# A new hand-written program order for one-core block-sparse attention followed by a gated feed-forward layer

## The chip, the cores and the metric

The kernel runs on 1 core of one Trainium2 chip. The metric is device time in microseconds for one execution. The kernel before takes 278.68 us (median of 3 runs, 277.92 to 278.79).

## The reference

The input is q, k and v in float32, each (4 batches, 8 heads, 768 positions, 64 dimensions), a table of three sampled key blocks for each of 24 query blocks, and three weights. Attention is dense in its arithmetic and masked by blocks of 32; the feed-forward layer reads the attention output as 3072 tokens of 512 features.

```python
scores = (1/8) * q @ k.T
mask = |blk_i - blk_j| <= 1  or  first/last block row or column  or  sampled block
attn = softmax(where(mask, scores, -1e9)) @ v        # (4, 8, 768, 64)
x = attn.transpose(0, 2, 1, 3).reshape(3072, 512)
gate = sigmoid(x @ w_gate)                           # w_gate, w_val: 512 x 1536
out = (gate * (x @ w_val)) @ w_out                   # w_out: 1536 x 512
```

All of it is computed. The sigmoid is taken as a tanh of half the argument, and the factor 1/2 is applied when the output leaves PSUM. Masked scores are made zero after the exponential by a product with a 0/1 mask, except for the first unit, where a bias is added by matmuls before the exponential.

## The kernel before

**Tiling.** The work has 12 units: batch b (0 to 3) by a third u of the queries (256 queries). A unit has 4 pairs of heads. For each pair there are three steps of 256 keys each:

- `scores` on TensorE: 4 matmuls of 64x128 weights (kT) by 256 columns of qT, two in parallel on the two halves of the array's rows; in the first unit 8, with the bias.
- `exp` on ScalarE: 128x1024 elements out of PSUM, to a buffer P.
- `mul` on VectorE: P times the mask (not in the first unit).

Then `pv` (units 0 and 1, whole array, 24 matmuls) or `pv_parts` (later units, half the rows each, 48 matmuls) forms P times v with a column of ones for the sum; `fold` (VectorE) adds the two halves, `norm` (VectorE) divides. The result is transposed to xT, for units 0 and 1 by TensorE with a copy out of PSUM (`turn`, `evac`), later by a DMA transpose from SP's queue (`xbar`).

The feed-forward part has 8 groups of units. A task `f` makes 512 columns of gate and value: a first half and a second half of 16 or 8 matmuls each (the first group in one piece on the whole array), then `tanh` on ScalarE and `gate` on VectorE, which frees the PSUM unit. A task `y` makes 256 output tokens in six parts of 8 matmuls, two evacuations and two stores from SP's queue. The last unit's output (`y_last`) is split in three so that the last evacuation is small.

**Preparation.** Batch 0's k and q come in as two heads at a time, are transposed by TensorE and copied out of PSUM by VectorE or ScalarE (`prep.turn`, `prep.evac`); the block mask is expanded by small matmuls (`mask_tiles`) and copied to SBUF. Later batches are loaded on POOL's queue, paired on VectorE (`pair_up`) and transposed by DMA on SP's queue; v is copied to a padded buffer on VectorE (`vcopy`). The first loads stand in a fixed list, `FIRST`, and are not touched here.

**Order.** All engines' programs follow from one list, `ORDER`. Every piece of work is a task with a number; `Plan.run` goes through the tokens and issues each task's instructions on its engine. A token is a task number, an optional engine letter (P, A, D, G, S) that replaces the task's first choice, `:n`, which of the four PSUM units it takes, and `@m`, a gate: this load waits until task m has run. `jN` is a filler of two matmuls on zeros into unit N (`jNs` a short one). Each engine runs its own instructions strictly in this order; semaphores come from data and buffers. There are four PSUM units of two banks, and a task that takes a unit waits until the evacuation of its last owner is done. So a token's place decides three things: what is behind it on its engine, when a unit comes free, and when a load starts.

The task numbers that the prediction speaks of are: 126, 127, 132, 133, 147, 171, 176, 190 (f of the first group); 204 to 206 (first y); 34, 32, 44, 40, 36, 30, 64, 56, 60, 46, 50, 54 (scores of the first unit); 38, 48, 58, 93 (their pv); 14, 19, 24, 29 (their v copies); 15/16, 17/18, 20/21, 22/23, 25/26, 27/28 (transposes of batch 0 and their copies); 74 to 85, 97/98, 106/107, 117/118 (mask matmul and its copy); 138/139 and 152/153 (pair copy and DMA transpose of k and q of batch 1, pair 0), 229/230 (k of pair 2); 268 and 318 (scores of batch 1, pairs 0 and 2); 1148 to 1157 (y of unit 10), 1158 to 1172 (y_last); 1097 and 1099 (the stores of unit 9's output).

Of the kernel before, what the change touches and what calls it, by code (L numbers as in the profile page):

```python
# [24 lines left out]
DM = H * D  # L25
# [20 lines left out]
122:3 85A 113 140:0 127 123 91 130:1 128 132:3 141 129 131 72:2 119:0 99:1 73D 133 120 147:2 134  # L46
100 135 142 157:0 148 154:3 171:1 124 155 149 158 88 164:3 143:2 156 176:0 92@164 144 121 146@111
101 172 170@44 165 173 161:2 217@54 145 190:1 177 189@46 162 125@40 178 237@54 159 186:3 191 150:2
115:0 151D 192 174:2 187 116 204:1 175 188 231:0 179:3 183:2 232 205 180D 244:3 184 233 206 166
245 82:0 200:2 218 83D 201 246 234:3 193:0 219 194A 152 235 185 153 211:2 136:0 220 137D 212 138  # L50
272:3 195 139 229 223A 202 167:0 255:2 168 236 273 213 221A 239 214:0 230 307:1 274 169 215 275
256 240 216 197:3 308 257 196 181 198 258 248:0 309 182 199 241:2 249 242 310 268:3 262 225:1 250
260 114@268 263 269 251 252:2 226 318:0 261 207:3 319 253 315:1 208 289:2 316 160@315 254 106:0
265:3 243 290 107A 247@265 266 270 276:1 209 291 300:0 293:3 277 301 278 282:1 294 292 283 297 163
303:0 335:2 295 302 222 304 279 227 285:1 336 296 286 238 359:0 305 337 360 210 284 331:3 228
362:1 348 332 361 264 349 363 333 328:0 287 350 329 267 322:3 351A 320 344:1 353A 311:0 323
203@344 345 341:2 387:3 321@359 312 342 317 271@282 426:1 373:0 313 411@300 427 330 397:2 374 398
343 388 346 375 259 408:1 376 389 355:2 400@268 409 390 347@30 419:0 356 334@89 380:3 405:1 428
370:2 381 306@111 364 420 288@44 406 371 386@214 366:3 421 410 365@265 454:2 422 433:1 455 432@380
# [3 lines left out]
442 474:1 484:0 463A 378 465A 339 467:2 452 340 475 524:3 480 485 525 514 354 515:1 327 468 486  # L63
# [4 lines left out]
538 583 438 550:1 567 571 542 439 586 551 638:0 563:2 572 425 539 564 552 595:1 573A 404 577:2 604  # L68
639 574 596 578 609:0 568 597 555 575A 627:2 598 616:3 610 628 617 543@616 635:1 565 712@200 630:2
611 569@300 636 612 592:3 446@563 688:0 631 593 658@60 689 654 706:1 556@231 588:3 707 579 641@550  # L70
640 642:0 632 676@471 619:1 633 589 587@282 620 594 691@214 623:2 690 613 590 670:1 591 643 671
637 605:3 624 644 621 606 645 659:1 618 625 709:0 681:3 710 626 660 607 655:2 682 692:0 656 453
663:3 711 726@99 661 657 608@234 673:2 693 662 674 622@652 664 672 694 548 699:1 695 665 723:2 666
# [3 lines left out]
762 669 782 730:3 745A 734:0 760 757:2 731 735 753 798:3 703 758 799 732 736 764:0 759 750 743A  # L77
600 765 797 826:3 823:1 767 763 824 650 816:0 766 651 827 809:1 756 768 810 719 800 787:3 817 769
733 788 806:1 801:0 807 770D 819:3 789 772A 811 737:1 790:2 839 738 614 802 580 615 791 803 601
# [5 lines left out]
904 856 925 936:0 978:1 913 937 911 857 919:3 979 908 875:0 920 914 876 929:1 921 917A 905 932  # L85
970:3 930 935 971 877 922 946:0 915A 1024:3 931 947 893 1025 928 1027:2 1012:0 939 938 916 1013
948 959:3 1028 966 1040:0 940 960 1041 1026 941 967:2 973:3 944A 942D 968 945 1029 952:0 1001:1
# [6 lines left out]
1078 1074 1094 1008 1082 1095 1083 1084 1100:1 1087A 1096A 1108:3 1088 1098A 1101 1085A 1099 1097  # L94
# [3 lines left out]
1163:2 1154D 1164 1159 1156D 1155 1157 1165 1160 1166 1167 1168:0 1161 1169 1170 1162 1171 1172  # L98
"""
GAP, PV_HALF, PV_PARTS, F_HALF, Y_ONE = 0.3, 0.36, 0.74, 0.875, 0.216  # L100
# [56 lines left out]
def kernel(  # L157
# [246 lines left out]
    t_mb = plan.add([(DVE, 0.7)], mask_blocks)  # L404

    def rows(c1, fn, engines):

        bank = Bank()

        def mm(eng):  # L410
            for i, c0 in enumerate(range(0, c1, 512)):
                c = slice(c0, min(c1, c0 + 512))
                nc.tensor.matmul(
                    both(bank)[:, i, 0 : c.stop - c0], mb16, e64[0:D, c], start=True, stop=True
                )

# [13 lines left out]
        [(DVE, 0.42)],  # L430
    )
    t_rows = [
        rows(S, lambda eng, spread: copy(eng, mb24, spread), [(DVE, 0.95), (ACT, 0.82)])
    ]

    def mask_tiles(c0, c1, j):
# [14 lines left out]
        def evac(eng):  # L451
# [3 lines left out]
        a = plan.add([(PE, n / 4800)], mm, t_rows, take=bank, ops=4)  # L455
        return plan.add(
            [(DVE, 0.12 + n / 860), (ACT, 0.16 + n / 1180)], evac, [a], free=bank
# [20 lines left out]
    def prep(nm, src, dst, b, p, t0, t1):  # L478
# [32 lines left out]
        if staged is None:  # L511
            c = plan.add([(PE, 0.04 * n)], turn, take=bank, ops=8 * n)
            copies.setdefault((nm, b, p), []).append(c)
        else:
            a = plan.add([(DVE, 0.1 + 0.14 * n), (ACT, 0.2 + 0.14 * n)], pair, before("pr", i))
# [7 lines left out]
    def pair_up(nm, src, dst, b, p, deps):  # L523
        def go(eng):
            nc.vector.tensor_copy(
                dst[:, p, :, :, :],
                src[:, 2 * p : 2 * p + 2, :, :].rearrange("a h t d -> a t h d"),
            )

        a = plan.add([(DVE, 0.36)], go, deps)  # L530
        copies.setdefault((nm, b, p), []).append(a)
        return a

# [624 lines left out]
```

## Time and profile before

| | |
|---|---|
| runs | 277.92, 278.68, 278.79 us |
| profiled execution, span from first to last instruction | 277.8 us (the page gives no other time of it) |
| mean granted clock of TensorE | 0.999 |
| TensorE busy | 270.0 us (97%) |
| VectorE busy | 207.1 us (75%) |
| ScalarE busy | 192.1 us (69%) |
| POOL busy (issuing loads) | 47.3 us (17%) |
| DMA | 28.93 MB, mean 104 GB/s |

In the profile PE is TensorE's matmul, PEld its weight load, DVE VectorE, ACT ScalarE. A row names the source line, the engine, the operation and its tiles. Matmuls overlap: a row's length is from issue to the modelled end, so two rows that start 0.11 us apart may each be 0.27 long, and TensorE's pace is read from starts. A table by windows has for each stretch its length, then the busy time of each engine, and at the end the granted clock, the mean share of DMA and GB/s. In a timeline the columns are start and length in us; square brackets hold the engine's idle time before the row and what ended it.

### The profile page before, as it was taken

To read this page: it belongs to the slowest core of one execution; us is meant where nothing else is said; L and a number is where in the kernel's file an instruction comes from. 1 tells how busy PE (TensorE), PEld (TensorE's weight loads), DVE (VectorE), ACT (ScalarE), POOL (GpSimd) and SP (SyncE) were. 2 spreads that over 40 slices of the span, in tenths; PEclk is the share of its full clock that TensorE was granted. 3 is DMA by queue.
4 is the path that set the end of the run, shared out by engine and by line. 5 is a ranking of instruction groups with operands and counts; after the bars stand their busy time and mean duration, and the time that the engine had idled before them with its cause. 6 is when DMAs were issued, how large, how long until landed. Compare 5 with 4: busy or idle time off the path is not lost.

```text
span 277.8 us, 11169 instructions
## 1 busy us (share of the span) xinstructions
PE 270.0 (97%) x5007; PEld 178.7 (64%) x5007; DVE 207.1 (75%) x421; ACT 192.1 (69%) x243; POOL 47.3 (17%) x69
## 2 busy tenths in 40 slices
PE   8879999999999999999999999999999999999995
PEld 3667785896897798655566655655655676555543
DVE  4667788899999989978988886887876899004422
ACT  3988868899989958968868965679688571035300
POOL 7776261030480000028300000000000000000000
PEclk9999999999999999999999999999999999999999
DMA  7999999994599693339986743014130002230004
GB/s 160 175 195 197 200 205 198 140 139 100 84 160 145 117 140 97 103 98 167 142 113 113 73 61 97 2 21 142 24 96 4 4 2 76 70 151 2 0 2 151
DMA packets 56684, 28.93 MB, mean 104 GB/s; under 512 B 33036, under 2 KB 53692, under 8 KB 56636
## 3 DMA queue, kind: packets, MB, share of 16 engines
q0 software_dynamic: 21520, 13.90, 35.7%
q1 hardware_dynamic: 34628, 14.02, 24.8%
q8 instruction: 39, 0.64, 1.0%
q10 hardware_dynamic: 488, 0.30, 0.3%
q14 instruction: 9, 0.07, 0.1%
HBM read 28.47 MB, written 6.29 MB: 125 GB/s over the span
## 4 chain that ended last, share of the span: by engine, by line
PE 87%; DMA 7%; POOL 2%; ACT 1%; DVE 1%; issue 1%; SPq 0%
PE m L352 86%; DMA q<-in_q_dram 3%; DMA v<-in_v_dram 2%; DMA kT<-kp 1%; ACT P L586 1%; POOL k L226 1%; POOL q L226 1%; POOL wg L236 0%; POOL wv L236 0%; DVE ysb L888 0%; DVE P L592 0%; ACT ysb L886 0%; PE m L472 0%; PE m L467 0%; ACT ysb L929 0%
## 5 line engine op out<-in xcount | busy, mean ns | idle before, releaser
L586 ACT ACTIVATE P<-m 128x1024 f16<-128x1024 f32 x144 | 143.1, 1025 | 27.8 <-PE m L352 24.6
L352 PE MATMUL m<-xT,wg 64*128 64x512 f16 (+2 forms) x720 | 136.7, 326 | 0.1
L352 PE MATMUL m<-xT,wv 64*128 64x512 f16 (+2 forms) x720 | 136.7, 326 | 0.0
L592 DVE TENSOR_TENSOR P<-P,mask 128x1024 f16<-128x1024 f16 x132 | 87.0, 684 | 2.7 <-ACT P L586 2.6
L352 PEld LDWEIGHTS <-wg 64*128 64x128 f16 (+1 forms) x720 | 66.6, 94 | 21.2 <-issue 0.8
L352 PEld LDWEIGHTS <-wv 64*128 64x128 f16 (+1 forms) x720 | 66.4, 94 | 18.2 <-issue 0.5
L804 DVE SCALAR_TENSOR_TENSOR ht<-th,m 128x512 f16<-128x512 f32 x72 | 49.0, 685 | 37.0 <-ACT th L801 36.1
L352 PE MATMUL m<-wo,ht 64*128 64x512 f16 (+2 forms) x564 | 70.4, 372 | 0.0
L801 ACT ACTIVATE th<-m 128x512 f32<-128x512 f32 x72 | 42.8, 598 | 29.6 <-PE m L352 26.1
L352 PE MATMUL m<-qT,kT 64*128 64x256 f16 x576 | 53.6, 269 | 0.9 <-DMA kT<-kp 0.5
L352 PEld LDWEIGHTS <-P 64*128 64x128 f16 (+1 forms) x2112 | 41.1, 94 | 5.2 <-issue 0.4
L352 PEld LDWEIGHTS <-ht 64*128 64x128 f16 (+1 forms) x564 | 29.4, 94 | 23.4 <-issue 1.3
L352 PE MATMUL m<-vex,P 64*128 64x65 f16 (+1 forms) x2112 | 42.5, 190 | 0.0
L352 PEld LDWEIGHTS <-kT 64*128 64x128 f16 x576 | 26.7, 94 | 17.8 <-issue 1.3
L646 DVE TENSOR_REDUCE acc<-m 128x260 f32<-128x520 f32 x40 | 27.8, 697 | 7.9 <-PE m L352 6.8
L226 POOL DMA_DIRECT2D k<-in_k_dram x15 | 11.1, 744 | 48.3 <-PE m L352 45.0
L886 ACT ACTIVATE ysb<-m 128x512 f32<-128x512 f32 x18 | 10.2, 601 | 11.8 <-PE m L352 11.8
L656 DVE TENSOR_TENSOR x<-acc,rz 128x256 f16<-128x256 f32 x40 | 17.0, 425 | 1.4
L226 POOL DMA_DIRECT2D v<-in_v_dram x16 | 11.6, 736 | 33.5 <-PE m L352 12.9
L226 POOL DMA_DIRECT2D q<-in_q_dram x19 | 13.9, 733 | 3.9 <-DMA wo<-in_moe_w_out_dram 1.8
L352 PE MATMUL m<-bias,e 64*128 64x256 f16 x48 | 5.9, 271 | 2.3 <-DVE mask L299 1.9
L929 ACT ACTIVATE ysb<-m 128x256 f32<-128x256 f32 x1 | 0.4, 383 | 10.1 <-PE m L352 10.1
(47 smaller groups left out, 84.1 us busy)
## 6 DMA issues: line engine op xcount, KB each, us to landing
out_dram<-ysb SPq DMA_DIRECT2D x23, 256.0 KB, 2.4
v<-in_v_dram POOLq DMA_DIRECT2D x16, 192.0 KB, 5.1
k<-in_k_dram POOLq DMA_DIRECT2D x15, 192.0 KB, 6.6
q<-in_q_dram POOLq DMA_DIRECT2D x12, 192.0 KB, 6.4
wg<-in_moe_w_gate_dram POOLq DMA_DIRECT2D x6, 256.0 KB, 8.4
wv<-in_moe_w_val_dram POOLq DMA_DIRECT2D x6, 256.0 KB, 9.0
wo<-in_moe_w_out_dram POOLq DMA_DIRECT2D x3, 512.0 KB, 12.8
xT<-x SPq DMA_TRANSPOSE x40, 2.4
```

The source lines that it names most:

```text
L226: return nc.gpsimd.dma_start(dst[:, h0:h1, t0:t1, :], src[b, h0:h1].rearrange("h (p t) d -> p h t d", t=NT)[:, :, t0:t1, :],)
L352: return nc.tensor.matmul(out, lhsT, rhs, start=start, stop=stop, skip_group_check=True).ins
L586: nc.scalar.activation(self.pt.rearrange("a h i n -> a (h i n)"), both(self.bank).rearrange("a h n -> a (h n)"), AF.Exp, bias=0.0, scale=SCALE
L592: nc.vector.tensor_tensor(self.pt, self.pt, m.unsqueeze(1).broadcast_to([128, 2, 2, UQ]), op=ALU.mult,)
L646: nc.vector.tensor_reduce(self.acc.rearrange("a h s d -> a (h s d)"), self.parts.rearrange("a r n -> a n r"), axis=mybir.AxisListType.X, o ...
L656: nc.vector.tensor_tensor(self.x16.rearrange("a s h d -> a h s d"), self.acc[:, :, :, 0:D], rz.broadcast_to([128, 2, 2, D]), op=ALU.mult,)
L801: nc.scalar.activation(th, both(bank)[:, 0, :], AF.Tanh, bias=0.0, scale=0.5)
L804: nc.vector.scalar_tensor_tensor(self.ht[:, tiles[0] : tiles[-1] + 1, :], in0=th.rearrange("a (f n) -> a f n", n=self.w), scalar=1.0, in1= ...
L886: nc.scalar.activation(ysb, both(bank)[:, s, :], AF.Copy, bias=0.0, scale=0.5)
L929: nc.scalar.activation(ysb, src, AF.Copy, bias=0.0, scale=0.5)
```

## The change

Only `ORDER` changes what runs: the order of all engines, the PSUM unit of each task, the engine of some copies and the gates of the loads are new. The tasks themselves, and so the matmuls, exponentials, products, copies, loads and stores, are the same. Beside it, the numbers for durations and the labels in the `plan.add` calls are replaced; they are notes for whoever writes the order, and `Plan.run` reads none of them but the engine letter of the first choice and the bank to take.

Counted in the two lists: filler pairs go from 19 to 13. Output evacuations go from 18 on ScalarE and 4 on VectorE to 14 and 8; mask copies from 3 and 6 to 2 and 7; transposed copies of xT in the first units from 1 and 7 to 3 and 5; copies of k and q in the first batch from 1 and 12 to 2 and 11, and the 768-column mask rows go from VectorE to ScalarE. All 36 later loads have a gate in both. The changes of the array's tile shape along TensorE's order are 43 in both.

```diff
 ORDER = """
-j3 j3 j3 j3 j3 j3 j3 j3 5A 8D j3 0 11A j3s 9:0 j3s j3s j3s 10D j3s j3s 12:1 1:2 j3s 13A 3:0 2 j3s 34:1 4D 35 15:2
-j3s 32:3 16D 6:0 33 17:1 7D 117:2 18D 97:0 118D 44:1 98A j3s 22:3 78:2 23D 45 36:0 79D 20:3 37 21D
-40:2 25:1 30:3 41 26D 76:0 77D 46:1 31 54:2 19 74:0 47 75D 27:3 24 55 50:0 28D 80:1 64:3 51 81D
-48:2 65 60:1 49 56:0 61 14 66:3 58:2 67D 105@30 57 29 89:3 59 38:1 90 52:0 86:2 53D 87 39 68:3
-93:0 69D 62:1 108:2 94 42:3 109 43D 102:0 63D 111:3 70:1 103 110 126:2 71D 112 104 95:0 84:1 96D
...
-1115 1126 1136:0 1127 1117 1121 1118 1132:1 1122 1137 1123 1119 1128:3 1138 1133 1139 1144:2 1134
-1140:0 1135 1129 1145 1130 1141 1131 1146 1148:1 1147 1142 1149 1143 1150 1158:3 1151 1152 1153
-1163:2 1154D 1164 1159 1156D 1155 1157 1165 1160 1166 1167 1168:0 1161 1169 1170 1162 1171 1172
+0 5A j3 j3 j3 j3 j3 j3 j3 j3 j3s 6:0 11 8A j3s j3s 9:1 10 12:2 1:3 2 13 7A 3:0 4A j1s j1s 15:3 16A
+34:2 84:0 85 92@34 32:1 17:3 18 97:0 35 98 33 44:3 45 22:2 23 78:0 40:1 41 25:2 79 36:0 37 27:3
+30:1 28 26 74:3 75 31 64:2 65 20:0 21 76:3 77 56:1 57 14 60:0 46:2 47 38:3 19 39 48:1 50:2 61 49
+51 42:3 29 54:0 55 43 66:1 67 93:3 24 86:1 80:2 87 105@86 99:0 100 94 81 58:3 167:1 168 217@167 59
+82:2 83 68:0 146@167 69 164:3 165 95:2 96 52:1 53 102:0 62:2 63 111:1 108:3 126:2 103 166 109 112
+70:0 71 127 89:3 128 129 90 140:0 141 132:1 113 119:3 120 72:2 104 133 134 122:0 73 237@122
...
+943 1096D 1082 1083 1084 1085 1087 1104:0 1116:1 1086 1105 1106 1107 1117 1118 1098D 1124:2 1128:0
+1140:3 1129 1141 1119 1130 1131 1142 1143 1100:1 1112:0 1101 1108:3 1113 1102 1103 1114 1132:1
+1088 1115 1109 1110 1111 1125 1120:0 1136:3 1121 1126 1127 1144:2 1133 1122 1123 1134 1135 1137
+1138 1139 1145 1146 1148:1 1149 1147 1150 1163:2 1151 1152 1153 1156 1157 1164 1158:3 1154 1097
+1159 1160 1165 1161 1099 1162 1155 1168:1 1169 1170 1171 1172 1166 1167
 """
```
```diff
-        a = plan.add([(PE, c1 / 2200)], mm, [t_mb], take=bank, ops=2 * (1 + (c1 > 512)))
+        a = plan.add([(PE, c1 / 2400 + 0.003)], mm, [t_mb], take=bank, mode="Q", needs=("c0", "e0"))
...
-        return plan.add([(SP, 1.25)], go, deps, dma=("T", 0))
+        return plan.add([(SP, 1.29)], go, deps, dma="T")
...
-                [(ACT, 0.98)], st.exp, [a] + before("P", 3 * pr.i + st.j), free=st.bank
+                [(ACT, 0.903)], st.exp, [a] + before("P", 3 * pr.i + st.j), free=st.bank
```

More of the change, by code (lines that the diff above doesn't have):

```diff
@@ L429 @@
         ),
-        [(DVE, 0.42)],
+        [(DVE, 0.335)],
     )
     t_rows = [
-        rows(S, lambda eng, spread: copy(eng, mb24, spread), [(DVE, 0.95), (ACT, 0.82)])
+        rows(S, lambda eng, spread: copy(eng, mb24, spread), [(DVE, 0.87), (ACT, 0.70)])
     ]
@@ L454, in mask_tiles @@
         n = 2 * (c1 - c0)
-        a = plan.add([(PE, n / 4800)], mm, t_rows, take=bank, ops=4)
+        a = plan.add([(PE, n / 4800 + 0.003)], mm, t_rows, take=bank, needs=("e0", "e1"))
         return plan.add(
-            [(DVE, 0.12 + n / 860), (ACT, 0.16 + n / 1180)], evac, [a], free=bank
+            [(DVE, 0.065 + n / 960), (ACT, 0.054 + n / 1200)], evac, [a], free=bank
         )
@@ L548, in go @@
             )
-        a = plan.add([(DVE, 0.4)], go, deps + read.get(("pv", b - 2, p), []))
+        a = plan.add([(DVE, 0.268)], go, deps + read.get(("pv", b - 2, p), []), needs=(f"v{p}",) if b == 0 else ())
         copies.setdefault(("v", b, p), []).append(a)
@@ L692, in value @@
                 a, free = plan.add(
-                    [(DVE, 0.66)], self.fold, [a] + folded[-3:-2], free=self.bank
+                    [(DVE, 0.609)], self.fold, [a] + folded[-3:-2], free=self.bank
                 ), None
             self.normed = plan.add(
-                [(DVE, 0.6 if free else 0.5)], self.norm, [a] + before("x16", self.i), free=free
+                [(DVE, 0.55)], self.norm, [a] + before("x16", self.i), free=free
             )
@@ L722, in xt @@
                 plan.add(
-                    [(DVE, 0.29), (ACT, 0.37)],
+                    [(DVE, 0.203), (ACT, 0.268)],
                     self.evac,
@@ L744, in scores @@
         a = plan.add(
-            [(PE, (0.44 if first else 0.22) * len(run))],
+            [(PE, (0.433 if first else 0.217) * len(run))],
             mm,
@@ L748, in scores @@
             take=run[0][1].bank,
-            ops=16 if first else 8,
+            score=True,
+            needs=("e0", "e1") if first else (),
         )
@@ L758, in scores @@
                 continue
-            pr.products.append(plan.add([(DVE, 0.66)], st.mul, [e] + masks[st.j, st.u]))
+            pr.products.append(plan.add([(DVE, 0.599)], st.mul, [e] + masks[st.j, st.u]))
         return a
@@ L844, in f @@
                     take=bank,
-                    lag=GAP,
-                    ops=16 * self.per,
+                    needs=wneeds,
                 )
                 a = plan.add(
-                    [(PE, F_HALF)], half(False), [a], ops=16 * self.per
+                    [(PE, 0.863 if self.w == 512 else 0.872)], half(False), [a], turn=True
                 )
             used["xT"][self.g].append(a)
-            c = plan.add([(ACT, 0.57)], tanh, [a] + before("th", i), free=bank, part=1)
-            g = plan.add([(DVE, 0.68)], gate, [c], free=bank, part=1)
+            c = plan.add([(ACT, 0.477)], tanh, [a] + before("th", i), free=bank)
+            g = plan.add([(DVE, 0.598)], gate, [c], free=bank)
             used["th"][i] = [g]
@@ L898, in part @@
                     take=bank if first and f0 == 0 else None,
-                    lag=0.0 if f0 < 8 else GAP if first else None,
-                    ops=16,
+                    turn=not first and f0 == 0,
+                    needs=(f"o{f0 // 4}",),
                 )
@@ L911, in y @@
                 e = plan.add(
-                    [(ACT, 0.6), (DVE, 0.69)],
+                    [(ACT, 0.477), (DVE, 0.605)],
                     lambda eng, s=s: evac(eng, s),
@@ L940, in store @@
                 [after],
[L941 removed]
+                dma="O",
             )
```

122 lines of the change are left out of this document (58 added, 64 removed), and 40 rows, old and new, of the table ORDER.

## The prediction

> **What bounds the kernel now.** I read, in this order, the page's shares and chain, the table by windows, the chain in order of time, and then the timelines of TensorE, ScalarE and VectorE for the first 25 us. The page first: TensorE's busy share and its share of the chain that ended last.
>
> ```profile
> PE 270.0 (97%) x5007; PEld 178.7 (64%) x5007; DVE 207.1 (75%) x421; ACT 192.1 (69%) x243; POOL 47.3 (17%) x69
> PE 87%; DMA 7%; POOL 2%; ACT 1%; DVE 1%; issue 1%; SPq 0%
> L586 ACT ACTIVATE P<-m 128x1024 f16<-128x1024 f32 x144 | 143.1, 1025 | 27.8 <-PE m L352 24.6
> ```
>
> TensorE is the bound, and the change leaves its work alone. So a new order can win only where TensorE waits. The windows (length in us, then busy time of each engine) show where that is.
>
> ```profile
> 4.60:16.00 11.40, 8.90 (x223) 6.59 (x221) 8.04 (x18) 8.88 (x11) 9.50 (x14) 1.00 1.31 178
> 16.00:24.00 8.00, 7.48 (x203) 5.83 (x201) 5.35 (x17) 7.22 (x8) 5.43 (x8) 1.00 1.45 197
> 42.00:110.00 68.00, 68.00 (x1628) 54.87 (x1624) 62.17 (x128) 59.54 (x74) 11.47 (x16) 1.00 0.88 132
> 110.00:125.00 15.00, 14.47 (x308) 8.95 (x302) 12.54 (x26) 12.17 (x16) 1.52 (x3) 1.00 0.38 100
> 125.00:200.00 75.00, 75.00 (x1404) 44.21 (x1402) 63.09 (x127) 56.80 (x71) 7.81 (x11) 1.00 0.54 87
> 200.00:210.00 10.00, 9.88 (x150) 5.72 (x146) 7.91 (x14) 8.67 (x11) 0.00 (x0) 1.00 0.24 74
> 265.00:277.80 12.80, 9.68 (x76) 5.01 (x70) 2.73 (x5) 0.38 (x1) 0.00 (x0) 0.98 0.22 83
> ```
>
> From 42 to 200 us TensorE rests only once, 0.53 us in all, and once more between 200 and 210. The rest of its idle time lies in the first 24 us (2.50 and 0.52) and in the tail (3.12, of which about 3.1 is the last evacuation and store). Busy hides something: a row's time includes the pipeline's drain, so starts must be read as well. The chain in order of time names the two waits in the middle and the end.
>
> ```profile
> 114.71 2.86 ACT P L586 x3
> 117.60 0.69 DVE P L592
> 118.29 0.28 DVE vex L545
> 118.66 4.07 DMA kT<-kp
> 204.92 0.60 ACT ysb L886
> 205.55 0.70 DVE ysb L888
> 274.71 0.38 ACT ysb L929
> ```
> ```profile
> 121.35 0.90 PE L352 MATMUL m<-vex,P 64*128 64x65 f16 x48
> 122.78 0.39 PE L352 MATMUL m<-qT,kT 64*128 64x256 f16 x3 [0.53 <-DMA kT<-kp]
> ...
> 205.80 0.38 PE L352 MATMUL m<-qT,kT 64*128 64x256 f16 x4
> 206.30 0.37 PE L352 MATMUL m<-xT,wg 64*128 64x512 f16 x1
> ```
>
> At 118 us a transpose of k for the next batch is issued late, behind VectorE's queue, and its landing at 122.7 holds the scores of task 616. At 205 us two evacuations of one output unit run one behind the other, and FFN half 1001, which takes that unit, waits for the second. The second fence gives TensorE's own starts there. The 48 value matmuls at 121.35 take 0.73 where the next task follows at once, so 1.43 - 0.73 = 0.70 is lost; the score at 205.80 takes 0.22 of its 0.50, so 0.28 is lost.
>
> **The start, step by step.** The timeline of ScalarE, then VectorE and TensorE, in the first 25 us (start, length, instruction, idle time before it):
>
> ```profile
> 6.73 1.94 ACT L586 ACTIVATE P<-m 128x1024 f16<-128x1024 f32 x2 [0.86 <-PE m L352]
> 8.56 0.59 ACT L297 CAST mask<-m 128x512 f16<-128x512 f32 x1
> 9.17 5.69 ACT L586 ACTIVATE P<-m 128x1024 f16<-128x1024 f32 x6
> 16.01 4.82 ACT L586 ACTIVATE P<-m 128x1024 f16<-128x1024 f32 x5 [1.15 <-PE m L352]
> 22.61 2.85 ACT L586 ACTIVATE P<-m 128x1024 f16<-128x1024 f32 x3 [0.55 <-PE m L467]
> ```
> ```profile
> 6.42 0.27 PE L352 MATMUL m<-qT,kT 64*128 64x256 f16 x2
> 6.62 0.38 PE L472 MATMUL m<-const,k 64*64 64x64 f16 x24
> 14.35 0.36 DVE L545 COPY vex<-v 128x768 f16<-128x768 f16 x1 [1.53 <-DMA v<-in_v_dram]
> 15.36 0.29 PE L352 MATMUL m<-bias,e 64*128 64x256 f16 x2 [1.91 <-DVE mask L299]
> 15.47 0.29 PE L352 MATMUL m<-qT,kT 64*128 64x256 f16 x2
> 16.47 0.79 PEld L352 LDWEIGHTS <-P 128*128 128x128 f16 x24 [0.21 <-issue]
> 23.94 0.28 PE L352 MATMUL m<-xT,wg 128*128 128x256 f16 x1
> 41.20 0.39 PE L352 MATMUL m<-wo,ht 64*128 64x512 f16 x2
> ```
>
> Six exponentials in 5.69 us, the last 1.025 long, are (5.69 - 1.03) / 5 = 0.93 us apart. A pair of 256-column matmuls starts 0.11 after the one before (15.36, 15.47), so a score costs 0.22 and a score of the first unit, with its bias, 0.44. A change of tile shape costs about 0.1 (weights at 16.47, 0.11 later than the pairs' pace); both orders have 43 of them, so they drop out. The before order puts the copy of v for pair 1 (19) on VectorE ahead of a mask copy (75). The v load was late, VectorE waited 1.53 us, the mask copy kept its PSUM unit, and TensorE waited 1.91 us at task 50. The first FFN task (126) begins at 23.94.
>
> The new order moves the v copies (14, 19, 29, 24) behind all mask copies that hold a unit, so this wait goes. What is late next is ScalarE. It gets two larger copies ahead of the first exponential (4A, the 768-column mask rows, and 16A, the transposed k of pair 1, whose transposes ran at 6.62 before), about 0.7 us each by the 0.59 that the 512-column copy takes. I walk it through: first exponential at 7.6 instead of 6.73; 16 exponentials at 0.93 are 14.9; and about 0.5 of idle time, because score 50 waits for the unit of exponential 47 behind two value products (38, 48). The sixteenth (165) then ends at 7.6 + 14.9 + 0.5 = 23.0. Task 108, which takes its unit, costs 0.2 and the hand-over and change of tile shape 0.1: task 126 starts at 23.3, 0.64 earlier. Ahead of it TensorE has also done more: scores 99, 167, 164, masks 82 and 84 and a transpose (0.93 us) come in, score 89, mask 117 and the transpose 70 (0.58) go out. So the lead is 0.64 + 0.35 = 1.0 us there. Up to the first output task (204) part of it is given back: scores 119 and 122 and FFN task 147 take units whose exponentials (90, 141, 120) end only as TensorE arrives. Counted in start-to-start lengths, 204 has 29.63 us of TensorE work ahead of it in the new order and 28.83 in the old; my walk puts it at 41.35 against 41.20: a lead of 0.80 - 0.15 = 0.65. I take **-0.65**; the ends are 0, if ScalarE idles 0.65 more, and -1.6, if its 0.5 of idle time and the hand-backs vanish. That the fillers fall from 19 to 13 pairs costs nothing: they run where TensorE waits anyway.
>
> **The middle.** The k and q transposes of later batches are reached with 10 to 50 us of TensorE work to spare (the tightest, 393, 10.7; before, 439 had 9.9 and was the one that stalled), and the unit after an output's evacuations (801, 387) is taken with 0.4 to 0.5 us to spare. Both waits, 0.70 and 0.28, go: **-0.98** (ends 0 and -1.04).
>
> Against that, the new order hands PSUM units over tighter. A score's matmul that starts at 6.42 has its partner at 6.53 and its exponential at 6.73: 0.20 of hand-over, then 1.025, so a unit can be retaken about 1.26 us of TensorE time after its score. In the new order eight takes lie at 1.29 (584 after 653, 524 after 496, and so on); before, none was under 1.5. Takes with less than 0.5 us to spare are 24 beyond the first 50 us, against 8. I walked 41 to 68 us with the rows' lengths and found the new order waiting 0.05 us in all; the slips must come from lengths that vary. I take **+0.3**; the ends are 0 and 24 x 0.1 = 2.4.
>
> Loads: all 36 keep a gate, at other places. POOL's queue gets batch 2's first load (271) behind score 186, about 44 us by my walk, where before it came behind the v load 203 and its gate 344, some 25 us of TensorE work later; VectorE's pair copies for it come earlier too. SP's queue then carries batch 1's transposes 139 and 153 at 44.4 and 45.8 us, while loads still run. The issue list gives their time to landing (median us at the end):
>
> ```profile
> xT<-x SPq DMA_TRANSPOSE x40, 2.4
> qT<-qp SPq DMA_TRANSPOSE x12, 4.2
> kT<-kp SPq DMA_TRANSPOSE x12, 3.3
> ```
>
> By 4.2 the second lands at 50.0, and score 268 wants it at 51.2; 230 is issued at 56.7, lands at 60.9 and is wanted at 62.3. Both hold, with 1.2 and 1.4 us to spare: 0. Copies that change engine (four output evacuations to VectorE, three masks and turns to ScalarE) lie beside TensorE and are priced in the hand-overs.
>
> The Trainium skill, page "DMA: Bandwidth & Descriptors", section "Queues, rings and completion order", says that each DMA engine goes round its queues packet by packet, so a transpose would share the engines with a running load and not wait for its end. By that rule the sum stays as it is; if a transpose waited for every load queued ahead of it, the rival "late transposes" below would come true. The trace agrees with the rule so far: 4.2 us for q, mostly under loads, against 2.4 for xT, where by the other reading the first would be as long as the loads last.
>
> **The tail.** The same nine whole-array tasks end it, with the same three changes of tile shape, then 1171 and 1172. Two older output stores (1097, 1099) are moved to SP's last microseconds, so that six stores follow one another in SP's queue from 4 us before TensorE's end on, instead of four. Output stores land between 1.7 and 4.4 us after issue:
>
> ```profile
> DMA to landing us min/median/max: 1.7/2.3/4.4
> ```
>
> The last evacuations also wait for those two stores to free their buffers, which they do about 1 us ahead. I take **+0.2** (ends 0 and +0.6).
>
> Sum: -0.65 - 0.98 + 0.3 + 0.2 = -1.1 us on the profiled span of 277.8, so 276.7. The page gives the profiled execution's span only; the median of the runs, 278.68, stands 0.9 above it, and the lowest, 277.92, 0.1. I take 0.9 for what lies around: **277.6 us**.
>
> **The rivals.**
> - *Slipping hand-overs* (the other side). Each of the 24 tight takes loses 0.1 us. Exponentials stood 0.92, 0.93, 0.95 and 0.91 apart in the four rows above, so a few in a row can slip that far. Price 2.4 in place of 0.3: 278.68 - 1.63 + 2.4 + 0.2 = 279.7. It decides from about 0.07 us per take, where the gain is spent. For it: at 75.00 us busy of 75 from 125 to 200, TensorE has nothing to take a slip with. Against: the slip lets ScalarE catch up, so neighbours don't all slip.
> - *Late transposes.* If 139 and 153 land only after all loads then queued, among them the three v loads that the new order lets go by 42 us (203, 160, 114), 192 KB or about 1.0 us each at the 197 GB/s of the second window, I estimate their landing at 53.5 and a wait of 2.3 us for score 268: 279.9. Against: 4.2 us above.
> - *A better start.* ScalarE without idle time and the lead kept: 276.6. For it: ScalarE idled 0.86, 1.15 and 0.55 before, and the 0.5 of my walk may be too much.
> - *Nothing comes of it.* New waits of the same size appear: 278.2 to 279.0. For it: the loads that the start waits for keep their order and so their landings.
>
> **How the numbers follow.** The forecast has 0.50 (its own range 276.9 to 278.2), slipping hand-overs 0.15, late transposes 0.07, a better start 0.15, nothing 0.13. 0.3% of the median, 0.84 us, is about what a measurement of this kernel can tell from no change. Of the forecast's half some 0.39 lie below 277.84 and the rest within; with the better start 0.54 are faster. Same are 0.11 of the forecast and most of "nothing", 0.22 with a mild slip. Slower are the slips, the late transposes and what is left of "nothing": 0.24. The range that leaves out no more than 2 in 10 runs from 276.3, the better start with a run as low as the fastest of before, to 279.8, the slips.
>
> **What would show it.** Task 126, the first 128x256 wg matmul, starts near 23.3 instead of 23.94; no wait of TensorE for a mask near 15; no wait for a k transpose beyond 60 us and no row of VectorE's output evacuation in the chain; TensorE idle under 0.5 us in all between 42 and 265. It is wrong if TensorE waits for exponentials show up as many gaps of 0.05 to 0.2 us there, if a transpose ends a wait near 51 or 62, if the first exponential comes later than 7.8, or if the last store lands more than 3.6 us after the last matmul.

## The result and the profile after

| | before | after |
|---|---|---|
| time, median (range) | 278.50 us (277.92 to 278.79, 4 runs) | 293.25 us (292.88 to 294.75, 4 runs) |
| profiled execution, span | 277.8 us | 291.2 us |
| mean granted clock | 0.999 | 0.987 |
| TensorE's last matmul to the end of the span | 3.1 us | 3.8 us |

The ratio is 1.0544 (95% interval 1.051 to 1.0578): slower by 14.75 us (293.25 - 278.50) where 1.1 us faster was forecast. The page first: engine shares, the share of the chain that ended last, and the exponentials.

```profile
PE 276.2 (95%) x4995; PEld 187.4 (64%) x4995; DVE 209.0 (72%) x422; ACT 191.5 (66%) x242; POOL 47.2 (16%) x69
...
PE 84%; DMA 5%; ACT 5%; DVE 3%; issue 2%; DVEq 0%
...
L585 ACT ACTIVATE P<-m 128x1024 f16<-128x1024 f32 x144 | 141.7, 1032 | 31.4 <-PE m L351 30.7
```

The exponentials are as long as before. TensorE is busy 6 us longer, though it runs 12 filler matmuls fewer and otherwise the same ones. In the chain ScalarE goes from 1% to 5%, VectorE from 1% to 3%, and "issue", which is time in which the engine waited for nothing that the profile shows, from 1% to 2%; the DMA's share falls from 7% to 5%. The table by windows (length, busy time of PE, PEld, DVE, ACT, POOL, then granted clock, DMA share, GB/s) says where. A DMA share adds up the times of all packets, so it can be above 1.

```profile
42.00:49.00 7.00, 7.00 (x134) 4.22 (x130) 6.45 (x14) 6.38 (x9) 3.58 (x5) 1.00 1.31 201
49.00:56.40 7.40, 3.58 (x125) 2.94 (x123) 4.47 (x10) 2.36 (x4) 0.00 (x0) 0.91 1.30 184
...
56.60:61.70 5.10, 5.10 (x51) 4.09 (x48) 1.20 (x3) 2.19 (x3) 1.02 (x2) 0.50 1.14 143
...
88.00:100.00 12.00, 9.54 (x236) 8.51 (x232) 8.99 (x19) 7.62 (x11) 2.86 (x4) 1.00 1.33 176
...
120.00:133.00 13.00, 12.55 (x272) 9.94 (x268) 10.83 (x23) 11.18 (x13) 0.72 (x1) 1.00 0.61 113
...
174.00:178.00 4.00, 3.49 (x85) 2.42 (x80) 3.74 (x9) 2.91 (x5) 0.00 (x0) 1.00 0.52 115
```

Between 49.0 and 56.4 TensorE rests for more than half of the time, and from 56.6 to 61.7 it is busy throughout but at half the clock. Before, the same microseconds had the full clock:

```profile
56.60:61.70 5.10, 5.10 (x220) 4.83 (x214) 4.77 (x10) 4.74 (x7) 2.09 (x3) 1.00 0.95 131
```

The counts of matmuls (51 and 220) are of different kinds of task and don't compare. Against before, read at equal amounts of TensorE work (each task at the shortest start-to-start length of its kind), the lag is 0.0 us after 30 us of work, 7.0 after 45, 10.7 after 80, 11.3 after 120 and 12.7 after 250; the tail adds 0.7, which makes the 13.4 between the spans. TensorE's timeline shows the stretch that costs 7 us:

```profile
51.41 0.27 PE L351 MATMUL m<-xT,wg 64*128 64x256 f16 x1
...
51.52 0.27 PE L351 MATMUL m<-xT,wg 64*128 64x256 f16 x1
51.55 0.27 PE L351 MATMUL m<-xT,wv 64*128 64x256 f16 x1
54.00 0.91 PE L351 MATMUL m<-vex,P 64*128 64x65 f16 x48 [2.18 <-ACT P L585]
54.72 0.29 PE L351 MATMUL m<-mb,e 64*128 64x256 f16 x2
56.22 0.61 PE L351 MATMUL m<-qT,kT 64*128 64x256 f16 x4 [1.21 <-DMA qT<-qp]
56.60 0.41 PE L351 MATMUL m<-xT,wv 64*128 64x256 f16 x1
...
56.82 0.41 PE L351 MATMUL m<-xT,wv 64*128 64x256 f16 x1
```

Product 225 waits 2.18 for an exponential, score 268 (the row at 56.22) waits for the transpose 153, and then a 256-column matmul of the same kind starts 0.22 after the last (56.60, 56.82) where it was 0.11 (51.41, 51.52). In windows of 0.2 us the granted clock is 1.00 up to 55.0, 0.50 from 55.2 to 61.8, and 1.00 again from 62.0. So it fell as the second wait began: the rest ahead of it is the 2.18 of product 225. Who held that exponential stands in the timelines of ScalarE and VectorE: the evacuation 221 waited for its twin, 223 on VectorE, with the exponential behind it, and 223 stood behind the fold 253 of a product that TensorE had only just finished.

```profile
52.44 0.60 ACT L884 ACTIVATE ysb<-m 128x512 f32<-128x512 f32 x1 [3.18 <-DVE ysb L886]
52.93 1.02 ACT L585 ACTIVATE P<-m 128x1024 f16<-128x1024 f32 x1
```
```profile
51.05 0.70 DVE L645 TENSOR_REDUCE acc<-m 128x260 f32<-128x520 f32 x1 [1.06 <-PE m L351]
51.66 0.68 DVE L886 TENSOR_SCALAR ysb<-m 128x512 f32<-128x512 f32 x1
```

The transpose is in the chain in order of time, and in the DMA queues of the stretches 45.4 to 49.0 and 49.4 to 55.0 us (packets, MB, and their added-up times as a share of the 16 engines' time):

```profile
46.73 9.35 DMA qT<-qp
```
```profile
q0 software_dynamic: 985, 0.71, 129.5%
q8 instruction: 1, 0.02, 1.7%
```
```profile
q0 software_dynamic: 861, 0.62, 71.4%
q1 hardware_dynamic: 1474, 0.37, 58.0%
```

The transposes 139 and 153 are issued at 45.3 and 46.7, but q1, their queue, moves no packet at all until 49.0. But for one packet of q8, all goes to q0, the loads that POOL issued before and just after them. The first packet of q1 starts at 49.3, 4.0 us after the issue of 139. Part of that is no wait for loads: in before three q transposes that were issued with q1 idle had their first packet 1.2 to 1.3 us later, two of them with no load on the engines and one with loads still running. From 49.3 on the two queues share the engines, and the transposes land at about 55.5 and 56.1, when the last of these loads does.

Four gaps of TensorE have no releaser, and they lie inside tasks, between instructions that need nothing new. They are called code gaps below, for the reason that follows.

```profile
20.61 0.83 PE L351 MATMUL m<-vex,P 128*128 128x65 f16 x22 [0.80 <-issue]
...
50.58 0.36 PE L351 MATMUL m<-vex,P 64*128 64x65 f16 x12 [0.43 <-issue]
...
91.55 0.27 PE L351 MATMUL m<-xT,wv 64*128 64x256 f16 x1 [1.01 <-issue]
...
96.65 0.33 PE L351 MATMUL m<-vex,P 64*128 64x65 f16 x10 [1.32 <-issue]
```

Windows from gap to gap count what TensorE ran between them:

```profile
20.30:50.40 30.10, 29.29 (x512) 21.49 (x512) 24.70 (x51) 24.64 (x31) 14.28 (x20) 1.00 1.35 200
50.40:91.00 40.60, 36.21 (x766) 30.44 (x766) 31.96 (x69) 30.71 (x38) 10.74 (x15) 0.92 1.15 143
91.00:96.00 5.00, 3.77 (x128) 3.66 (x128) 3.44 (x8) 3.09 (x5) 1.43 (x2) 1.00 1.35 181
```

Matmuls and weight loads together are 1024, 1532 (and four semaphore instructions) and 256: multiples of 256. The page's DMA table has a queue for code:

```profile
q8 instruction: 39, 0.64, 0.9%
```

39 packets of 16 KB for some 10,000 instructions of TensorE are again about 256 instructions each. One of them ends shortly before each gap does: at 19.3, 49.1, 90.1 and 95.4, which is 1.2 to 1.5 us before TensorE goes on at 20.6, 50.6, 91.6 and 96.7. So TensorE's program arrives in blocks, and it stops at a block's edge when the next block is late. The Trainium skill, page "Runtime: NRT & Kernel Launch", section "Instruction fetch mechanics", says the same of the size, 16 KiB or 256 instructions, and that the cost of a boundary is mostly hidden; here the four gaps show 3.6 us of it.

### The profile page after: what moved, and what is told of

Same layout as the page of the kernel before. It is cut to its first block, busy times and chain, and to the rows that moved or that the text cites. A ratio compares the mean times of both kernels' runs of the same rounds, so it can differ in the third digit from the quotient of the medians.

```text
span 291.2 us, 11151 instructions
## 1 busy us (share of the span) xinstructions
PE 276.2 (95%) x4995; PEld 187.4 (64%) x4995; DVE 209.0 (72%) x422; ACT 191.5 (66%) x242; POOL 47.2 (16%) x69
## 4 chain that ended last, share of the span: by engine, by line
PE 84%; DMA 5%; ACT 5%; DVE 3%; issue 2%; DVEq 0%
PE m L351 83%; ACT P L585 4%; DMA qT<-qp 3%; DMA k<-in_k_dram 2%; DVE ysb L886 1%; ACT ysb L884 1%; DVE acc L645 1%; PE m L471 1%; DVE mask L298 0%; DVE x L655 0%; PE m L466 0%; DVE kT L298 0%; ACT ysb L926 0%; DVE rz L654 0%; DVE e L206 0%
## 5 line engine op out<-in xcount | busy, mean ns | idle before, releaser
L351 PE MATMUL m<-xT,wv 64*128 64x512 f16 (+2 forms) x720 | 139.1, 331 | 1.0 <-issue 1.0
L351 PE MATMUL m<-xT,wg 64*128 64x512 f16 (+2 forms) x720 | 138.7, 331 | 1.1 <-ACT ysb L884 0.5
L591 DVE TENSOR_TENSOR P<-P,mask 128x1024 f16<-128x1024 f16 x132 | 85.6, 684 | 10.3 <-ACT P L585 10.1
L351 PE MATMUL m<-qT,kT 64*128 64x256 f16 x576 | 55.4, 272 | 1.8 <-DMA qT<-qp 1.2
L351 PEld LDWEIGHTS <-ht 64*128 64x128 f16 (+1 forms) x564 | 31.3, 94 | 23.2 <-issue 1.1
L351 PEld LDWEIGHTS <-kT 64*128 64x128 f16 x576 | 29.4, 95 | 16.1 <-issue 3.5
L884 ACT ACTIVATE ysb<-m 128x512 f32<-128x512 f32 x14 | 8.0, 609 | 19.4 <-PE m L351 14.0
L886 DVE TENSOR_SCALAR ysb<-m 128x512 f32<-128x512 f32 x8 | 5.5, 688 | 6.3 <-DMA out_dram<-ysb 3.7
L654 DVE RECIPROCAL rz<-acc 128x4 f32<-128x4 f32 x40 | 6.9, 173 | 0.5
```

Source lines behind the costliest of these rows:

```text
L351: return nc.tensor.matmul(out, lhsT, rhs, start=start, stop=stop, skip_group_check=True).ins
L591: nc.vector.tensor_tensor(self.pt, self.pt, m.unsqueeze(1).broadcast_to([128, 2, 2, UQ]), op=ALU.mult,)
L654: nc.vector.reciprocal(rz, self.acc[:, :, :, D : D + 1])
L884: nc.scalar.activation(ysb, both(bank)[:, s, :], AF.Copy, bias=0.0, scale=0.5)
L886: nc.vector.tensor_scalar(ysb, in0=both(bank)[:, s, :], scalar1=0.5, scalar2=None, op0=ALU.mult)
```

## The experiments

Each edit is in `ORDER` alone. Ratios are to the kernel before, on the same chip.

**1. Four loads later.** The loads that ran ahead of the transposes 139 and 153 wait for score 268.

```diff
-203@241 ... 160@241 ... 114@244 ... 138 271@186
+268:3 203@268 160@268 114@268 271@268
```

> The changed kernel with four loads moved: the v loads 203, 160, 114 and the first load of batch 2 (271) are let go only after score 268. Theory (late transposes): in the changed kernel the transpose 153 was issued at 46.73 and landed at 56.09, together with the last of these loads, and score 268 waited for it. Without the four loads ahead of it, it lands within about 5 us, near 52, as in the kernel before (4.87); score 268 then starts near 54, set by the product 225 that waits for ScalarE, TensorE has no second idle stretch, the granted clock stays at 1.00 between 56 and 62 us: 293.25 - 2 - 3.2 = 288. Rival (the wait of ScalarE for VectorE's output evacuation is the root): score 268 still starts near 56 and the time stays at 292.5 to 293.5. Rival (code supply): as the theory, but the gaps inside tasks 434 and 401 (1.3 and 1.5 us) stay in both cases.

Measured: 297.89 us, ratio 1.0678 (1.0595 to 1.0762), slower than the changed kernel. The first half held: the transposes 139 and 153 landed 6.0 and 5.3 us after their issue, and no wait for them is left at score 268. But the wait of 225 and the drop of the clock stayed (0.79 and 0.67 in the windows 49 to 56 and 56 to 62), and the loads met the next transposes: score 318 waited for a k transpose.

```profile
74.37 0.61 PE L350 MATMUL m<-qT,kT 64*128 64x256 f16 x4 [5.39 <-DMA kT<-kp]
```

So loads do delay transposes, wherever they meet. Moving four of them in one bunch only moves the place.

**2. Evacuations not split.** All six output units whose halves went to two engines are evacuated by ScalarE.

```diff
-223D 221 ... 353 ... 351D ... 573 ... 575D ... 745 ... 743D ... 770D 772 ... 915D 917
+223A 221 ... 353 ... 351A ... 573 ... 575A ... 745 ... 743A ... 770A 772 ... 915A 917
```

> The changed kernel with all six split output evacuations on ScalarE (223, 351, 575, 743, 770, 915 moved from VectorE to ScalarE). Theory (the two halves of an output unit, evacuated by two engines, run one after the other, and the engine that comes second holds its whole queue): the waits of ScalarE for VectorE's evacuation (3.18 at 49, 0.83 at 175, 1.43 at 211) and of VectorE for ScalarE's (0.42 at 80, 1.48 at 130) go, and with them TensorE's gaps behind them: 0.55 at task 408, 0.7 at 592 and 655, 0.69 at 826, 0.5 at 930 and 946, together about 2.4; the wait of 225 (2.2) goes too, but score 268 still waits for the transpose until about 56, so the stretch up to it gains nothing: 290.9. Rival (ScalarE is too full for six more evacuations of 0.6 us): the same gaps come back as waits for exponentials, 292.5 to 294.

Measured: 293.51 us, ratio 1.0514 (1.0452 to 1.0576): no change. The wait of 225 went, as expected, and score 268 waited for 153 all the longer. TensorE's waits:

```profile
PE m L350 <- DMA qT<-qp: 4.2, 2, 4.0
PE m L350 <- issue: 3.7, 4, 1.7
```

The gaps at 408, 592, 826 and 930 went too, but smaller ones came at 638 and 894, and the code gaps stayed (3.7 us in all for 3.6). Against the 290.9 expected, one of two overlapping waits taken away gave nothing.

**3. Fillers in the idle stretch.** Matmuls on zeros keep TensorE busy; nothing else moves.

```diff
-236 225:1 117:2 118A 268:3
+236 j2 j2 j2 j2 j2 j2 j2 j2 j2 225:1 117:2 118A j3 j3 j3 j3 j3 j3 268:3
```

> The changed kernel with filler matmuls on zeros in the two idle stretches: nine pairs ahead of product 225 and six ahead of score 268. Nothing else moves. Theory (the granted clock fell to 0.51 between 56 and 62 us because TensorE had stood idle): TensorE keeps busy, the clock stays at 1.00, and the matmuls of 256 columns that took 0.21 apiece take 0.11 again: 293.25 - 3.2 = 290. Rival (those tasks are slow for another reason, such as the transposes that run beside them): the clock stays low, 293.

Measured: 290.85 us, ratio 1.0441 (1.0371 to 1.0510). The windows 49 to 58 and 58 to 64:

```profile
49.00:58.00 9.00, 6.66 (x154) 4.42 (x152) 4.07 (x9) 2.10 (x3) 0.00 (x0) 1.00 1.31 155
58.00:64.00 6.00, 6.00 (x114) 5.98 (x112) 3.65 (x10) 4.77 (x7) 1.75 (x3) 1.00 1.06 175
```

The clock stays at 1.00, and tasks 256 and 272, the two FFN halves behind score 268, take 0.87 each, though the same transposes run beside them. So the half pace was the clock, which had followed TensorE's rest; the median is 2.4 us lower, although 153 landed 1.7 us later still in the profiled execution. The 60 added instructions also move the edges of the code blocks, and the code gaps fall from 3.6 to 0.5 us. So how much of the 2.4 is the clock's is not shown.

**4. Code blocks shifted by 128 instructions.** 32 more short filler pairs where TensorE waits for the first loads.

```diff
-0 5A j3 j3 j3 j3 j3 j3 j3 j3 j3s 6:0 11 8A j3s j3s 9:1 ... 4A j1s j1s 15:3
+0 5A (28 x j3s) j3 j3 j3 j3 j3s 6:0 11 8A (6 x j3s) 9:1 ... 4A (6 x j1s) 15:3
```

> The changed kernel with 32 more short filler pairs in the first 6 us, where TensorE waits for loads: each pair is four instructions, so every later instruction stands 128 places later in TensorE's program. Theory (TensorE's program comes in blocks of 256 instructions by DMA, and a block that comes late behind the loads is the cause of the gaps at 19.36, 49.72, 90.02 and 94.89, which stand 1024, 1532 and 256 instructions apart): the gaps inside tasks 434 and 401 go, and gaps of 0.5 to 1.5 us appear, if at all, 128 instructions earlier or later in the order, again a multiple of 256 apart; the packet of 16 KB still ends 1.2 to 1.5 us before each gap ends. The time changes by -2 to +1. Rival (the gaps belong to those tasks, say to a wait that the profile does not show): they stay inside tasks 434 and 401 with the same length, 293.3.

Measured: 291.80 us, ratio 1.0434 (1.0369 to 1.0500), 1.5 below the changed kernel. (The expectation's times of the gaps stand 0.9 to 1.8 us ahead of the rows above.) No gap is left inside tasks 434 and 401, where the gaps at 91.6 and 96.7 were, and no code gap anywhere. A wait that belonged to those tasks would have stayed. The profile is of the longest execution, 297.1, which has another wait, of 3.5 us for a transpose of x near 108, and a second fall of the clock there (0.57 from 106 to 114).

**5. Loads one by one.** 24 loads of later batches, which the new order lets go early and in bunches, are let go one by one.

```diff
-203@241 ... 160@241 ... 114@244 ... 271@186 ... 432@268 ... 446@359 347@359 608@359
+268:3 203@268 ... 160@282 ... 114@341 ... 271@380 ... 432@300 ... 446@408 ... 347@495 ... 608@498
```

> The changed kernel with 24 loads of later batches let go later, one by one, each at least 5 us ahead of the copy that reads it (203 behind score 268 and 160, 114, 321 and so on behind later scores; 386 to 691 between 92 and 139 us of the changed kernel's time). Nothing else moves. Theory (loads let go early keep the DMA engines full, so that transposes and TensorE's code come late): 153 lands about 5 us after its issue, the transposes for score 318 too, no code gap inside tasks 434 and 401; what is left is the 2.4 us that product 225 waits for ScalarE and the drop of the granted clock behind it: 293.25 - 1.3 - 3 = 289. Rival (the loads only collide with other transposes, as when four of them were moved): a wait of several us for a transpose appears elsewhere, 293 or more.

Measured: 292.12 us, ratio 1.0494 (1.0454 to 1.0534). 289 was expected. The transposes 139 and 153 landed 6.6 and 5.8 us after issue, in time for score 268, and the gaps inside 434 and 401 went; but code gaps of 0.45 and 0.98 stay at 20.3 and 50.8, 225 still waited 2.19 for ScalarE, and the clock fell during that wait to 0.50 for about 3.4 us. Then the same with all evacuations on ScalarE:

> The same later loads, and all six split output evacuations on ScalarE. Theory (three causes: late transposes, late code, and ScalarE held by VectorE's evacuation; the drop of the clock follows from the idle stretch that the first and the third make): TensorE no longer rests around 50 to 56 us, the granted clock stays at 1.00 there, 256 and 272 take 0.87 each: 293.25 - 6.9 - 2.7 - 1 = 282 to 284. Rival (loads alone are enough, the evacuations cost nothing by themselves): the same time as with the loads alone.

Measured: 288.87 us, ratio 1.0312 (1.0271 to 1.0353). The stretch is whole now:

```profile
49.00:56.00 7.00, 6.79 (x186) 5.88 (x182) 5.20 (x12) 5.33 (x10) 0.71 (x1) 1.00 1.07 135
56.00:62.00 6.00, 6.00 (x115) 5.94 (x111) 5.53 (x13) 5.48 (x8) 2.14 (x3) 1.00 1.18 153
```

Alone the two edits gave ratios of 1.0514 and 1.0494, both intervals overlapping that of the changed kernel (1.0544); together they give 1.0312, clear of it, and 4.4 us less by the medians. Each of the two waits at 54 us hid the other, and either was enough to bring the clock down: it fell in the profile where only the wait of 225 is left (experiment 5) and in the one where only that of 268 is (experiment 2), and not here. The gain is less than the 9 to 11 expected: 491 waited 1.8 us for a transpose of x that shares SP's queue and the engines with loads, and other small waits appeared.

**6. All that was found.** The last kernel with the fillers of experiment 4 and with the output stores 1097 and 1099 about 20 us earlier on SP's queue.

> The changed kernel with the later loads, all six split evacuations on ScalarE, the 32 short filler pairs at the start, and the output stores 1097 and 1099 about 20 us earlier on SP's queue. Theory (late transposes, late code, the held ScalarE and the tail are what was left out of the prediction, and they add up once none hides another): 288.87 with the first two undone, less 1 to 2 for code gaps near 87 and 91 us, less 0.4 for the tail: 286.5 to 287.5; what stays above the kernel before are waits for transposes of x and k, which share the DMA engines with 24 loads and SP's queue with each other. Rival (after the loads and evacuations nothing else matters): 288.5 to 289.5.

Measured: 286.32 us, ratio 1.0269 (1.0228 to 1.0311). The end of the span comes 3.5 us after the last matmul instead of 3.8. So the edits together undo 6.9 of the 14.75 us by the medians, about half, as by the ratios (2.75 of 5.44 points). Of the rest, TensorE's rows name 1.03 at 82.6 us, where VectorE's queue stands behind a q load that now comes too late, 0.94 for a transpose of x (task 491), 0.67 at product 322, 0.64 at a score near 24 us and a code gap of 0.63 at 18.3; none of these was tried, and what makes up the remainder stays open.

**7. The gates alone, in the old order.** The kernel before with only the four loads of experiment 1 let go as early as in the changed kernel.

```diff
-114@268 ... 160@315 ... 203@344 ... 271@282
+231:0 203@231 160@231 114@231 ... 138 271@231
```

> The kernel before with the four loads 203, 160, 114 and 271 let go at 42 to 48 us, as in the changed kernel; nothing else moves. Theory (the gates do the harm by themselves: loads queued ahead of the transposes of batch 1 delay them by about one us for each load): the transposes 153 and 139 land near 55 instead of 51 to 52, score 268, which wants them at 55.9 here, waits 0 to 1 us, the transposes behind them are late by 2 to 4 us and at least one further score or product waits: 279.5 to 283 against 278.5. Rival (the harm needs the new order, which wants score 268 at 51): 278.2 to 279.0.

Measured: 283.74 us, ratio 1.0138 (1.0096 to 1.0180): slower by 1.4%, clear of no change, or 4.6 us by the medians. The transposes 153, 139 and the next one land 8.9 to 10.3 us after issue, where q and k transposes took 3.3 to 4.9 there before. TensorE's two largest new gaps:

```profile
56.33 0.39 PE L352 MATMUL m<-qT,kT 64*128 64x256 f16 x4 [1.41 <-DMA kT<-kp]
...
58.67 0.88 PE L352 MATMUL m<-vex,P 64*128 64x65 f16 x30 [0.94 <-issue]
```

Both mechanisms appear in the old order, with nothing changed but when four loads start: late transposes, and a late block of code. The granted clock falls too, to a mean of 0.86 and 0.89 in the windows 56 to 60 and 60 to 70. So loads let go early do harm by themselves.

**8. The split alone, in the old order.** Five more evacuations of the kernel before on VectorE (`223D`, `351D`, `575D`, `743D`, `915D`).

> The kernel before with five more evacuations on VectorE (223, 351, 575, 743, 915), so that the same six output units as in the changed kernel are split over two engines. Theory (a split pair makes one engine's queue wait for the other's): two to four waits of 0.3 to 1 us of one engine for the other, and 0.5 to 2 us more in all: 279.0 to 280.5 against 278.5. Rival (a split is harmless as long as neither engine is behind): 278.2 to 278.8.

Measured: 278.90 us, ratio 0.9989 (0.9974 to 1.0004): nothing. Its profile has one wait of ScalarE for VectorE's evacuation, of 0.6 us, where the changed kernel has three, up to 3.2. So the rival holds in the old order: the split is harmless where VectorE isn't behind. At 49 us of the changed kernel it was, behind the fold 253.

**9. The two gains that the prediction counted, in the old order.** First the copies of v behind the copies that free PSUM units:

```diff
-54:2 19 74:0 47 75D 27:3 24 55 50:0 28D 80:1 64:3 51 81D 48:2
+54:2 74:0 47 75D 27:3 28D 55 50:0 80:1 81D 64:3 51 19 24 48:2
```

> The kernel before with one thing of the new start: the copies of v, 19 and 24, stand on VectorE behind the copies 75, 28 and 81, which free PSUM units. Theory of the prediction's first step (the late v load held VectorE and TensorE by 1.9 us near 13): the wait for the mask copy goes, ScalarE's idle 1.15 us near 15 with it, and the code block needed near 19 still comes in time: 0.6 to 1.1 us faster, 277.4 to 278.0 against 278.5. Rival (what comes next at the start, a late block of code or ScalarE, takes it back, as in the changed kernel): 278.3 to 278.8.

Measured: 278.82 us, ratio 1.0013 (0.9991 to 1.0035): no gain. TensorE's wait for the mask copy near 14 us is 0.60 in its profile, and it is 0.60 as well in that of the next kernel, which keeps the v copies where they were; a value product now waits 0.69 for a v copy. Then the two waits of the middle:

```diff
-464 ... 466 ... 439 ... 425 ... 942D
+... 439 ... 425 464 466 ... 942
```

> The kernel before with its two waits of the middle taken away: the output stores 464 and 466 stand behind the transposes 439 and 425 on SP's queue, which so issue about 2 us earlier, and the evacuation 942 is done by ScalarE. Theory of the prediction's second step: no wait for a k transpose at 121 us (0.70) and none for VectorE's evacuation at 205 (0.28): 0.9 faster, 277.6 against 278.5. Rival (the work behind has no other slack, and the next late thing takes the place of these waits): 278.3 to 278.8.

Measured: 278.25 us, ratio 0.9983 (0.9964 to 1.0002). No change at all lies inside that interval. The same kernel in more executions:

> The kernel before with its two middle waits taken away (stores 464 and 466 behind the transposes 439 and 425, evacuation 942 on ScalarE) once more, to narrow the interval. Theory (the waits of 0.70 and 0.28 in the profile of before are in most executions): 0.3 to 0.5% faster. Rival (they are in some executions only, since the profiled one was about 1 us longer than the median): 0.1 to 0.2% faster.

Measured: 278.14 us, ratio 0.9968 (0.9950 to 0.9986). That interval covers both expectations. The chain, asked for from 100 to 260 us, is one piece, with both waits gone:

```profile
99.96 160.22 PE m L352 x2845
```

This kernel is the fastest of those run, 0.2 to 0.3% faster than before.

## Why the prediction was wrong

**The failed step** is in the middle: "By 4.2 the second lands at 50.0, and score 268 wants it at 51.2 ... Both hold ...: 0." It landed at 56.1, 9.35 us after its issue. The rival "late transposes" had this mechanism, with a chance of 0.07, and even it was too mild: a landing at 53.5 and 2.3 us. The 4.2 was a median over the twelve q transposes of before, and the reading "mostly under loads" was wrong: ten of the twelve have no packet of a load (q0) beside them in the 4.2 us behind their issue. So it was the price without loads, and the prediction put loads beside the transposes and kept it. The Trainium skill's rule on queues (page "DMA: Bandwidth & Descriptors", section "Queues, rings and completion order") was read as: a transpose shares the engines at once. The trace agrees from 49.3 us on (58.0% and 71.4%), but not before: the first packet of q1 came 4.0 us after the issue, where an idle q1 in before took 1.2 to 1.3 and the same transpose 2.5 to 2.6 with its loads moved (experiments 1 and 5). What delays it beyond that is not shown by any run here.

**What was left out altogether** are two prices that are paid only when something else is late. The clock: behind a rest of 2.18 us it fell to 0.50 for 6.8 us, 1.2 of which TensorE waited anyway, and the tasks from 268 to 273 took about 2.7 us longer than at full clock (256 and 272 alone take 0.87 each in experiment 3). And the code: the same full DMA engines that delay a transpose delay TensorE's next block. Counted back 256 rows from the gap that begins near 90.3, the block before was entered at 84.65; its successor's packet starts only near 89.1, and TensorE goes on 1.4 us after that packet's end. In before, near 77 us, a packet starts within about 1 us of the edge.

**The start** was right in its steps and wrong in its sum. ScalarE's first exponential comes at 7.77 (forecast 7.6), the mask wait is gone, and at 10 us of work TensorE is 1.5 us ahead. Then a block of code comes late (0.80 at 20.61), ScalarE idles 0.73 behind it, task 126 starts at 24.18 instead of 23.3, and at 20 us of work the lead is 0.03. So -0.65 came out at 0, its upper end. The v copies alone, in the old order, gave nothing either (experiment 9): the wait of 1.91 from which the gain was sized is 0.6 to 0.9 in the profiles of experiments 7 to 9 that keep this start.

**The two waits of the middle** were real, and taking them out of the old order gives 0.5 to 0.9 us, not always 0.98. The prediction sized them from one execution and put that execution at 0.9 below its time. In the runs since, time minus span is 1.8 (293.0 - 291.2), so the profiled execution of before took about 279.6 and was 1.1 above the median. With 1.8 in place of the 0.9, the prediction's own sum ends at 276.7 + 1.8 = 278.5, the median of before: no change, and not a gain.

**The hand-overs** (+0.3, and the rival "slipping hand-overs") did not fail as described: no string of gaps of 0.05 to 0.2 us behind exponentials, but single waits behind split evacuations (at tasks 408, 592, 826 and 930, 0.16 to 0.51 us of idle time in the rows), and the 2.18 of product 225. The prediction had put the evacuations that change engine "beside TensorE" and counted them in the 0.3.

**The tail** had the right sign: +0.7 for +0.2, beyond its upper end of 0.6. The two moved stores did not free their buffers the 1 us ahead that the prediction counted on:

```profile
DVE ysb L928 <- DMA out_dram<-ysb: 8.0, 1, 8.0
```

VectorE's last evacuations waited for a store's landing. Most of the 8.0 us is no loss: with the stores moved away (experiment 6) VectorE idles 7.6 at the same place, for TensorE. The difference of about 0.35 is what the tail got back there (3.5 for 3.8); the other 0.4 us of it stays open.

## What to carry to other kernels

A transfer's time to landing belongs to what is queued around it: when a change moves loads, every transfer behind them, TensorE's own code among them, has to be priced again at the loaded figure (here 9 us instead of 4). Waits that overlap hide one another, so experiments that undo one cause at a time can all show nothing, and only the pair shows the gain; and a rest of about 2 us costs more than itself when the clock falls behind it. Size a wait from several executions before counting its removal as a gain.

## What the hardware showed that was not expected

- TensorE's program comes in 16 KB packets of about 256 instructions, and with the DMA engines full of loads the next block was late by 0.4 to 1.3 us (3.6 us in four gaps, none in the profile of before).
- With loads queued, a transpose's queue moved its first packet 4.0 us after the first transpose was issued, against 1.2 to 1.3 in before, and the transposes landed 9 to 10 us after issue instead of 3 to 5.
- The granted clock fell to 0.50 for 6.8 us behind a rest of 2.18 us (with 0.43 of rest shortly before it), and for about 3.4 us during one of 2.19 in experiment 5; after a rest of 2.10, with fillers ahead of it (experiment 3), it stayed at 1.00. What decides between these is not shown. The Trainium skill, page "TensorE: Matmul & The Clock Gate", section "What's actually happening", names an idle window of about 3.4 us for this; the rest that brought the clock down in the changed kernel was shorter.
